# Sinkhorn-sorted attention and a max-out layer on one core: keys' block diagonal by accumulating selection matmuls, and another order of the first item's steps

## The chip, the cores and the metric

The kernel runs on one core of a Trainium2 chip. The metric is device time in microseconds (us), the median of several runs; before the change it is 168.74 us, with three runs from 168.64 to 168.83. The core has five engines that run their own instruction queues in order: TensorE (PE in the profile, with its weight loads as PEld), VectorE (DVE), ScalarE (ACT), GpSimd (POOL) and SyncE (SP). They meet through semaphores. Sixteen DMA engines move data between the chip's memory (HBM) and the on-chip memory (SBUF). Matrix products land in PSUM, which is divided here into four buffers of 128 x 1024 fp32.

## The reference

There are 4 batch items with 8 heads, 768 positions and 64 features a head. The positions are cut into 8 blocks of 96. A small matrix per head (8 x 8) is normalised by five Sinkhorn rounds, and the blocks of keys and values are mixed by it. Each block of queries then attends only to the mixed block of the same number. The result, as 3072 tokens of 512, goes through a max-out layer.

```python
P = sort_net                                   # 4 x 8 x 8 x 8
for _ in range(5):
    P = np.exp(P - max)                        # row maximum
    P = P / (P.sum(-1) + 1e-09)                # rows, then columns
    P = P / (P.sum(-2) + 1e-09)
k_sorted = einsum('bhij,bhjcd->bhicd', P, k_b) # the same for v
scores = scale * q_block @ k_sorted_block.T    # block by block
attn = softmax(scores)
x = (attn @ v_sorted_block)                    # -> 3072 x 512
out = np.maximum(x @ w1, x @ w2) @ w_out       # w1, w2: 512 x 1024
```

## The kernel before

**The max-out.** max(x w1, x w2) is written as relu(x (w1 - w2)) + x w2. So `w_difference` subtracts w2 from w1 in quarters of columns, `moe_h` makes g = relu(x (w1 - w2)) in four quarters t for each half `ch` of an item's tokens, and `out_products` adds g w_out and x (w2 w_out). The matrix w2 w_out (`wc`) is made once, by `w2_transposes` and `w_product`, during item 0.

**Sorting by matmul.** For one item the 8 x 8 matrices of 8 heads stand on a block diagonal of 64 x 64 (`bd_v` for values, `bd_k` for keys, both laid twice over 128 partitions). `sort_k` multiplies 16 columns c of keys at a time (three calls per item, 32 matmuls each), `sort_v` 16 features at a time (four calls for item 0, 16 matmuls each). Each call fills one PSUM buffer, which one copy of 1024 elements a partition evacuates, on ScalarE (L108) or VectorE (L110).

**The block diagonal.** After the last Sinkhorn round `p_bf` holds P for all 32 heads, one head a partition. `block_diagonals` spreads an item's rows to 128 partitions by one matmul with a selection of ones (`sel_k`, `sel_v`; L317), multiplies by a mask that keeps the wanted j (`maskJ`, into pm, L325), sums over j (pt, L332), and multiplies by a mask that keeps the head (`maskM`, into bd, L335). For item 0 keys and values go through these steps together. VectorE makes the selections, by copies of parts of the identity matrix.

**Per item**: `q_transposes` (two calls, 24 matmuls each), `scores` for 8 units u (8 matmuls, then an exp on ScalarE, L506), `values` for 8 units (8 matmuls, then a reciprocal and a multiply on VectorE into x, L536 and L542), four `x_transposes` (for item 0 on TensorE with an evacuation, later by DMA), eight `moe_h`, six output tiles. Units 0 to 3 belong to the first half of tokens and 4 to 7 to the second; a transpose of x takes two units.

**What sets the order.** All is in program order (a manual schedule). For item 0 the order up to `moe_h(0, 0, 1)` is written out by hand from `SC, VA, TR = att(0)` on. The rest of item 0, and the attention of the next item, run in a loop of units: each unit is one `moe_h`, `w_product` or half an output tile, and a table of tails (`first_tail` and so on) says which steps follow which unit. Where a step names no engine for its evacuation, `pick` gives it to ScalarE or VectorE by two running sums of cost. PSUM buffers are handed out in turn from the pool of four: a step waits until the buffer's last user has been read. `keep_streaming` puts matmuls of zeros ahead of a step to keep TensorE's clock up.

**Loads.** All loads of inputs but P go through GpSimd's queue, in program order: v, k and q of item 0, the weights in column pieces, then item 1's k and q, v of items 1 and 2, and so on. There are eight semaphores for them, used in turn, so the ninth load is issued when the first has landed. GpSimd also makes the identity matrix and the first two `w_difference` pieces (L205), which stand in its queue after the weight loads; the last two are VectorE's. `turn_v` puts V into the layout for sorting, on ScalarE (L222) or VectorE (L227).

Of the kernel before, what the change touches and what calls it, by code (L numbers as in the profile page):

```python
# [16 lines left out]
def kernel(  # L17
# [16 lines left out]
    nc = tc.nc  # L34
# [31 lines left out]
    def ps_f32(name):  # L66
        return psum.tile([128, 1024], FP32, tag="ps", name=name)
# [125 lines left out]
    make_identity(nc, ident)  # L193
    load_k(0)
    load_q(0, True)
    for t in range(2):
        load_w_columns(w2_sb, moe_w2, t, t + 1)
        load_w_columns(w1_sb, moe_w1, t, t + 1)
# [68 lines left out]
    def masks(part):  # L267

        if part == 0:
            nc.vector.tensor_tensor(  # L270
                out=id64, in0=ident[:, 0:64], in1=ident[:, 64:128], op=ALU.add
            )
            nc.vector.reduce_sum(
                out=maskJ[:, 0], in_=id64.rearrange("p (m j) -> p j m", j=NB), axis=AX.X
            )
            nc.vector.reduce_sum(
                out=maskM[:, 0], in_=id64.rearrange("p (m j) -> p m j", j=NB), axis=AX.X
            )
            return
        keys = id64.rearrange("p (a j ch) -> p a j ch", j=NB, ch=2)  # L280
        nc.vector.reduce_sum(
            out=maskJ[:, 1], in_=keys.transpose([0, 2, 1, 3]), axis=AX.XY
        )
        for ch in range(2):
            nc.vector.reduce_sum(
                out=maskM[:, 1, ch * 4 : ch * 4 + 4], in_=keys[:, :, :, ch], axis=AX.X
            )

    sel_v, sel_k = {}, {}

    def selections(b):
        heads = {0: (0, 1), 2: (2, 1), 3: (3, 3)}.get(b)
        if heads:
            sel_v[b] = const.tile([G, 2, 8, NB], BF16, tag=f"sel_v{b}", name="sel_v")
            for half, item in enumerate(heads):
                nc.vector.tensor_copy(
                    out=sel_v[b][:, half],
                    in_=ident[0:G, item * 8 : item * 8 + 8].to_broadcast([G, 8, NB]),
                )
        sel_k[b] = const.tile([G, 8, 16], BF16, tag=f"sel_k{b}", name="sel_k")  # L300
        nc.vector.tensor_copy(
            out=sel_k[b], in_=ident[0:G, b * 8 : b * 8 + 8].to_broadcast([G, 8, 16])
        )

    bd_v, bd_k = {}, {}

    def block_diagonals(kinds, m0=0):

        pe = ps_f32("pe")
        n = len(kinds)  # L310
        for c, (m, b) in enumerate(kinds):
            sel = (
                sel_k[b].rearrange("g h w -> g (h w)")
                if m
                else sel_v[b].rearrange("g two h j -> g (two h j)")
            )
            nc.tensor.matmul(  # L317
                pe[:, c * 64 : c * 64 + 64],
                sel,
                p_bf.rearrange("p i j -> p (i j)"),  # L320
                start=True,
                stop=True,
            )
        pm = const.tile([128, n, NB, NB], FP32, tag=f"pm{n}", name="pm")
        nc.vector.tensor_tensor(  # L325
            out=pm,
            in0=pe[:, 0 : n * 64].rearrange("p (m i j) -> p m i j", i=NB, j=NB),
            in1=maskJ[:, m0 : m0 + n].to_broadcast([128, n, NB, NB]).transpose([0, 1, 3, 2]),
            op=ALU.mult,
        )  # L330
        pt = const.tile([128, n, NB], FP32, tag=f"pt{n}", name="pt")
        nc.vector.reduce_sum(out=pt, in_=pm, axis=AX.X)  # L332
        for c, (m, b) in reversed(list(enumerate(kinds))):
            bd = const.tile([128, 8, NB], BF16, tag=f"bd{m}{b}", name="bd")
            nc.vector.tensor_tensor(  # L335
                out=bd,
                in0=maskM[:, m].to_broadcast([128, 8, NB]),
                in1=pt[:, c].to_broadcast([128, NB, 8]).transpose([0, 2, 1]),
                op=ALU.mult,
            )  # L340
            if m:
                bd_k[b] = bd.rearrange("p m i -> p (m i)")
            else:
                bd_v[b] = bd.rearrange("p m i -> p (m i)")


    v_sb = big.tile([BLK, 128, D + 16], BF16, tag="v_sb", name="v_sb")
# [169 lines left out]
    def values(b, u, n=0):  # L517
        ih, hp = divmod(u, HP)
        e = e_tiles.pop((b, u))
        m0 = (b % 2) * 64  # L520
        ps = ps_f32("o_ps")
        keep_streaming(ps, n)
        for h2 in range(2):
            for ii in range(4):
                nc.tensor.matmul(  # L525
                    ps[:, h2 * 512 + ii * 65 : h2 * 512 + (ii + 1) * 65],
                    e[:, (h2 * 4 + ii) * BLK : (h2 * 4 + ii) * BLK + 128],
                    v_sb[:, m0 + (hp + 4 * h2) * 8 + ih * 4 + ii, 0:65],
                    start=True,
                    stop=True,  # L530
                )
        ov = ps[0:BLK].rearrange("p (t f) -> p t f", t=2)[:, :, 0 : 4 * 65].rearrange(
            "p t (i f) -> p t i f", f=65
        )
        rs = xpool.tile([BLK, 2, 4], FP32, tag="rs", name="rs")
        nc.vector.reciprocal(out=rs, in_=ov[:, :, :, 64])  # L536
        if hp % 2 == 0:
            x_tiles[b, ih, hp // 2] = xpool.tile(
                [BLK, 2, 4, 2, D], BF16, tag="x", name="x", bufs=4
            )  # L540
        x = x_tiles[b, ih, hp // 2][:, :, :, hp % 2, :]
        nc.vector.tensor_tensor(  # L542
            out=x,
            in0=ov[:, :, :, 0:D],
            in1=rs.to_broadcast([BLK, 2, 4, D]),
            op=ALU.mult,
        )
        load["D"] += 900
# [70 lines left out]

    def moe_h_products(b, ch, t, hps, n=0):  # L620
        if hps[0] == 0:
            h_ps[t] = ps_f32("h_ps")
            keep_streaming(h_ps[t], n)
        for m in range(2):
            fb = t * 2 + m
            for hp in hps:
                nc.tensor.matmul(  # L627
                    h_ps[t][:, m * 512 : m * 512 + TCH],
                    w1_sb[:, hp, fb * 128 : (fb + 1) * 128],
                    xT[:, b % 2, ch, hp % 2, hp // 2, :],  # L630
                    start=(hp == 0),
                    stop=(hp == 3),
                )

    def moe_h(b, ch, t, eng=None, hps=(0, 2, 1, 3), n=0):
        moe_h_products(b, ch, t, hps, n)
        ps = h_ps[t]
        g = gpool.tile([128, 2, TCH], BF16, tag="g", name="g")
        src = ps.rearrange("p (t f) -> p t f", t=2)[:, :, 0:TCH]
        if (eng or pick((200 + 2 * TCH) / 1.2, (130 + 2 * TCH) / 0.96)) == "A":  # L640
# [62 lines left out]
    keep_streaming(ps_f32("fill_ps"), 86 * 142, most=142)  # L703
    for it in range(5):
        sinkhorn(it)
        if it < 2:
            masks(it)
        if it == 2:
            selections(0)
            turn_v(first, "A", 0, 18)  # L710
        if it == 3:
            turn_v(first, "A", 18, 36)
    turn_v(first, "A", 36, 56)
    turn_v(first, "A", 56, 80)
    block_diagonals([(0, 0), (1, 0)])
    turn_v(first, "D", 80, 96)

    SC, VA, TR = att(0)
    sort_k(0, 0, 1024, "A")
    sort_k(0, 1, 0, "D")  # L720
    sort_k(0, 2, 0, "A")
    sort_v(0, 0, 0, "D")
    sort_v(0, 1, 0, "A")
    q_transposes(0, 0, "D")
    sort_v(0, 2, 0, "A")
    sort_v(0, 3, 0, "D")
    SC[0]()
    SC[4]()
    q_transposes(0, 1, "D")
    SC[1]()  # L730
    VA[0]()
    SC[2]()
    values(0, 1, 512)
    SC[3]()
    values(0, 2, 512)
    x_transposes(0, 0, "A")
    VA[3]()
    VA[4]()
    SC[5]()
    moe_h_products(0, 0, 0, (0, 2), 512)  # L740
    x_transposes(0, 1, "A")
    SC[6]()
    VA[5]()
    moe_h(0, 0, 0, "A", (1, 3))
    SC[7]()
    VA[6]()
    moe_h(0, 0, 1, "A")
    x_transposes(0, 2, "A")
    w_difference(2)
    VA[7]()  # L750
    w2T_ready = w2_transposes(0, "D")
    w_difference(3)
    w2T_ready()
    for b in range(1, B):
        selections(b)
    for c, n, m in [(2, 2, 0), (4, 3, 1)]:
        nc.vector.tensor_copy(
            out=maskJ[:, c : c + n],
            in_=maskJ[:, m].to_broadcast([128, NB, n]).transpose([0, 2, 1]),
        )  # L760

    def turn(rows, c0):
        turn_v(rows, "D", c0, c0 + 24)
        load["D"] += 850

    load_q(1)
    for piece in range(2):
        for b in (1, 2):
            load_v(b, which=piece)
    load_k(2)  # L770

    def sorts_and_scores(b):
        SC, VA, TR = att(b)
# [4 lines left out]
    TQ = [lambda half=half: q_transposes(1, half) for half in range(2)]  # L778
    TURN = [lambda c=c: turn(both, c) for c in (0, 24, 48, 72)]
    first_tail = {  # L780
        2: [lambda: x_transposes(0, 3)],
        3: [lambda: w2_transposes(1, "A")(), lambda: load_q(2)],
        5: [lambda: block_diagonals([(0, 2), (0, 3), (1, 1), (1, 2), (1, 3)], 2)],
        7: KS,
        9: [TQ[0], TURN[0]],
        10: [SC[0], TQ[1], TURN[1]],
# [50 lines left out]
    }  # L837
    tails = [first_tail, second_tail, third_tail, {}]
    for b in range(B):
        units = [lambda t=t: moe_h(b, 0, t, None if b else "A") for t in range(4)]  # L840
        if b == 0:
            units[0] = lambda: None
            units[1] = lambda: None
        units += [lambda t=t: moe_h(b, 1, t) for t in range(4)]
        cost = [13] * 8
        if b == 0:
            units += [lambda dmt=dmt: w_product(dmt) for dmt in range(4)]
            cost += [17] * 4
# [45 lines left out]
```

## Time and profile before

Time 168.74 us; the profiled run's span is 166.8 us at a granted TensorE clock of 1.0. Busy time by stretch, from the trace:

| stretch, us | PE | DVE | ACT | POOL | what runs |
|---|---|---|---|---|---|
| 2 to 12 | 9.25 | 7.82 | 5.62 | 8.09 | Sinkhorn, zero matmuls, turning V, issuing loads |
| 12 to 20 | 7.04 | 6.80 | 6.63 | 4.03 | sorts and query transposes of item 0 |
| 20 to 25 | 4.38 | 4.01 | 3.24 | 4.50 | scores and values of item 0 |
| 25 to 30 | 4.74 | 3.18 | 4.38 | 2.95 | the same, with the first h products |
| 30 to 40 | 10.00 | 6.36 | 5.62 | 2.66 | h products of item 0 |
| 0 to 167 | 157.6 | 79.2 | 83.1 | 29.5 | all |

The columns give the microseconds in which an engine had an instruction running. Matmuls are pipelined and the records of their ends are modelled, so a full PE column says that TensorE had work at every moment, not that it ran at its peak. A chain of work, followed back from the last instruction, gives TensorE 82% of the span, VectorE 8%, ScalarE 3% and "issue" (an engine that waited for nothing the profile shows) 3%.

### The profile page before, as it was taken

The numbers are of one execution on the slowest core, as the hardware profiler recorded it, in microseconds if no ns is written. First come the engines' busy times: TensorE is split into PE (matmuls) and PEld (weight loads), VectorE is DVE, ScalarE is ACT, GpSimd is POOL, SyncE is SP. The second block draws the span as 40 slices with busy tenths as digits, with TensorE's granted clock in tenths as the row PEclk, the third lists the DMA queues.
The fourth block names the chain that finished last, engine by engine and source line by source line (L and its number), as shares of the span: only waits on it lengthen the run. The fifth ranks groups of instructions, "written<-read, shape, count | busy, mean of one in ns | idle before, by whom it ended". The sixth has DMA issues, their size and how long they took to land.

```text
span 166.8 us, 4537 instructions
## 1 busy us (share of the span) xinstructions
PE 157.6 (94%) x1993; PEld 95.7 (57%) x2011; DVE 79.2 (47%) x182; ACT 83.1 (50%) x101; POOL 29.5 (18%) x46
## 2 busy tenths in 40 slices
PE   7989799999999999999999999999999999999991
PEld 7839676766545555557555554575555545654451
DVE  4978885847484784535257774070642320000011
ACT  3587868674168627045752353467447206642010
POOL 7965587230113000000004120000000000000000
PEclk9999999999999999999999999999999999999999
DMA  3999999999999984659602999998025253000342
GB/s 43 205 205 197 199 207 206 211 203 218 207 202 215 216 219 87 173 111 173 133 0 57 160 221 169 202 250 84 2 51 173 47 173 130 0 0 0 126 155 102
DMA packets 30404, 23.90 MB, mean 143 GB/s; under 512 B 16752, under 2 KB 25200, under 8 KB 30384
## 3 DMA queue, kind: packets, MB, share of 16 engines
q0 software_dynamic: 11040, 13.37, 47.4%
q1 hardware_dynamic: 19200, 10.17, 27.1%
q8 instruction: 16, 0.26, 0.6%
q10 hardware_dynamic: 144, 0.07, 0.1%
q14 instruction: 4, 0.03, 0.1%
HBM read 26.75 MB, written 6.29 MB: 198 GB/s over the span
## 4 chain that ended last, share of the span: by engine, by line
PE 82%; DVE 8%; issue 3%; ACT 3%; DMA 1%; ACTq 0%
PE out_ps L654 34%; PE h_ps L627 25%; PE wc_ps L607 4%; PE k_ps L408 4%; PE o_ps L525 4%; PE s_ps L498 3%; PE tq_ps L383 2%; DVE x L542 1%; PE v_ps L473 1%; PE tw_ps L588 1%; ACT e L506 1%; DVE v_dc L227 1%; DMA p_sb<-in_sort_net_dram 1%; PE v_ps L429 1%; ACT xT L108 1%
## 5 line engine op out<-in xcount | busy, mean ns | idle before, releaser
L654 PE MATMUL out_ps<-wo_sb,g 128*128 128x512 bf16 (+2 forms) x187 | 46.0, 370 | 1.4 <-issue 0.9
L627 PE MATMUL h_ps<-xT,w_sb 128*128 128x384 bf16 x256 | 44.4, 326 | 0.3 <-ACT xT L108 0.3
L627 PEld LDWEIGHTS <-w_sb 128*128 128x128 bf16 x256 | 24.2, 98 | 16.1 <-issue 0.4
L506 ACT ACTIVATE e<-s_ps 96x768 bf16<-96x768 f32 x32 | 24.2, 806 | 14.9 <-PE s_ps L498 14.9
L641 ACT ACTIVATE g<-h_ps 128x768 bf16<-128x768 f32 x27 | 21.9, 811 | 17.0 <-PE h_ps L627 16.9
L654 PEld LDWEIGHTS <-g 128*128 128x128 bf16 x200 | 17.1, 97 | 15.8
L654 PE MATMUL out_ps<-wc,xT 128*128 128x512 bf16 (+2 forms) x98 | 24.7, 370 | 0.1
L108 ACT COPY o<-out_ps 128x1024 f32<-128x1024 f32 x9 | 9.1, 1012 | 28.3 <-PE out_ps L654 25.7
L542 DVE TENSOR_TENSOR x<-o_ps,rs 96x512 bf16<-96x512 f32 x32 | 22.0, 687 | 1.1
L654 PEld LDWEIGHTS <-xT 128*128 128x128 bf16 x100 | 9.6, 97 | 11.2
L525 PEld LDWEIGHTS <-e 96*128 96x128 bf16 x256 | 11.5, 97 | 5.5
L536 DVE RECIPROCAL rs<-o_ps 96x8 f32<-96x8 f32 x32 | 6.4, 201 | 16.7 <-PE o_ps L525 16.7
L689 DVE COPY o<-out_ps 128x512 f32<-128x512 f32 (+1 forms) x2 | 1.3, 626 | 27.6 <-PE out_ps L654 27.6
L525 PE MATMUL o_ps<-v_sb,e 96*128 96x65 bf16 x256 | 12.7, 193 | 0.0
L110 DVE CAST v_sb<-v_ps 96x1024 bf16<-96x1024 f32 x8 | 9.7, 1217 | 4.6 <-PE v_ps L473 3.5
L643 DVE TENSOR_SCALAR g<-h_ps 128x768 bf16<-128x768 f32 x5 | 4.8, 956 | 12.1 <-PE h_ps L627 12.1
L110 DVE CAST kT<-k_ps 128x1024 bf16<-128x1024 f32 x6 | 7.2, 1221 | 6.7 <-PE k_ps L408 6.7
L108 ACT CAST v_sb<-v_ps 96x1024 bf16<-96x1024 f32 x8 | 8.0, 1008 | 3.1 <-PE v_ps L473 1.7
L498 PE MATMUL s_ps<-qT,kT 64*128 64x96 bf16 x256 | 8.7, 204 | 0.5 <-DVE qT L110 0.4
L160 POOL DMA_DIRECT2D v_raw<-in_k_dram x3 | 2.5, 822 | 37.8 <-DVE rs L536 37.6
L498 PEld LDWEIGHTS <-kT 64*128 64x128 bf16 x256 | 6.0, 94 | 5.4 <-issue 2.2
L169 POOL DMA_DIRECT2D v_raw<-in_v_dram x11 | 5.9, 539 | 12.7 <-DVE v_dc L227 7.5
(85 smaller groups left out, 144.6 us busy)
## 6 DMA issues: line engine op xcount, KB each, us to landing
out_dram<-o SPq DMA_DIRECT2D x11, 512.0 KB, 3.0
v_raw<-in_v_dram POOLq DMA_DIRECT2D x8, 384.0 KB, 13.4
k_raw<-in_k_dram POOLq DMA_DIRECT2D x9, 256.0 KB, 10.0
w_sb<-in_moe_w_dram POOLq DMA_DIRECT2D x4, 256.0 KB, 10.1
w_sb<-in_moe_w_dram POOLq DMA_DIRECT2D x2, 512.0 KB, 11.1
wo_sb<-in_moe_w_out_dram POOLq DMA_DIRECT2D x2, 512.0 KB, 14.5
v_raw<-in_v_dram POOLq DMA_DIRECT2D x3, 256.0 KB, 4.9
q_raw<-in_q_dram POOLq DMA_DIRECT2D x4, 192.0 KB, 9.2
```

Source lines behind the costliest of these rows:

```text
L108: nc.scalar.copy(out=out_ap, in_=in_ap)
L110: nc.vector.tensor_copy(out=out_ap, in_=in_ap)
L408: nc.tensor.matmul(ps[r0 : r0 + 64, m * 64 : (m + 1) * 64], kv[r0 : r0 + 64, t * 16 + m, :], bd_k[b][r0 : r0 + 64, :], start=True, stop=True,)
L498: nc.tensor.matmul(ps[:, h2 * 512 + ii * 128 : h2 * 512 + ii * 128 + BLK], kT[b][rows, (hp * 8 + i) * BLK : (hp * 8 + i) * BLK + 128], rhs ...
L506: nc.scalar.activation(out=e[:, 0 : 8 * BLK].rearrange("p (t c r) -> p t c r", t=8, r=R), in_=ps[0:BLK] .rearrange("p (t f) -> p t f", t=8 ...
L525: nc.tensor.matmul(ps[:, h2 * 512 + ii * 65 : h2 * 512 + (ii + 1) * 65], e[:, (h2 * 4 + ii) * BLK : (h2 * 4 + ii) * BLK + 128], v_sb[:, m0 ...
L536: nc.vector.reciprocal(out=rs, in_=ov[:, :, :, 64])
L542: nc.vector.tensor_tensor(out=x, in0=ov[:, :, :, 0:D], in1=rs.to_broadcast([BLK, 2, 4, D]), op=ALU.mult,)
L607: nc.tensor.matmul(ps[:, 0:512], w2T[:, fb, dmt * 128 : (dmt + 1) * 128], wo_sb[:, fb, :], start=(fb == 0), stop=(fb == NFB - 1),)
L627: nc.tensor.matmul(h_ps[t][:, m * 512 : m * 512 + TCH], w1_sb[:, hp, fb * 128 : (fb + 1) * 128], xT[:, b % 2, ch, hp % 2, hp // 2, :], sta ...
L641: nc.scalar.activation(out=g, in_=src, func=AF.Relu)
L654: nc.tensor.matmul(dst, g_tiles[b, ch, m // 2][:, m % 2, off : off + 128] if m < NFB else xT[:, b % 2, ch, hp % 2, hp // 2, off : off + 12 ...
```

## The change

**The keys' block diagonal of item 0** is made by a function of its own, `block_diagonals_first`. For keys, eight matmuls accumulate into eight columns: the j-th takes column j of P (`p_bf[:, :, j]`) and a selection `one_j` that holds ones only for partitions of block j. The sum over j is thus done in PSUM, and one multiply by `maskM` gives bd. The values keep the way over pm and pt, after the keys' multiply. `one_j` is made by GpSimd: a memset of zeros and a copy of parts of the identity.

**The selections** of the other items move from VectorE, after the first h products, to GpSimd, ahead of the weight loads. Item 0's stays on VectorE. The mask sum for values' j moves from Sinkhorn's first round to its third, and the copies of masks for later items move ahead of item 0's sorts.

**The order of item 0** is a list of steps up to the last of its eight h products. The letter at the end names the evacuating engine (A or D), F puts 512 columns of zeros ahead of the next step; k, v, tq, SC, VA, tx, tw are the sorts, query transposes, scores, values, x transposes and w2 transposes; `h01a` is the first half of the products of half 0, quarter 1 (two of four contractions), `h01bA` the second half with the evacuation. The halves of the h products are interleaved with each other and with the values. The loads for items 1 and 2 stand inside the list, 26 steps before its end, and the load of item 2's queries after it. In the unit loop the eight h units of item 0 and three of the tails fall away, and the two cost sums start from fixed values.

```diff
+    for b in range(1, B):
+        selections(b)                      # now on GpSimd
+    one_j = const.tile([G, 8 * 130], BF16, tag="one_j", name="one_j")
+    nc.gpsimd.memset(one_j, 0.0)
+    nc.gpsimd.tensor_copy(
+        out=one_j.rearrange("g (j x) -> g j x", x=130)[:, :, 0:128].rearrange(
+            "g j (h w) -> g j h w", w=16
+        )[:, :, :, 0:2],
+        in_=ident[0:G, 0:8].to_broadcast([G, 8, 2, NB]).transpose([0, 3, 1, 2]),
+    )
...
+    def block_diagonals_first():
+        pe = ps_f32("pe")
+        for j in range(NB):
+            nc.tensor.matmul(pe[:, 0:NB], one_j[:, j * 128 : (j + 1) * 128],
+                             p_bf[:, :, j], start=(j == 0), stop=(j == NB - 1))
+        nc.tensor.matmul(pe[:, 512:576], sel_v[0], p_bf, start=True, stop=True)
+        # bd_k[0] = maskM[:, 1] * pe[:, 0:NB]
+        # pm = pe[:, 512:576] * maskJ[:, 0]; pt = sum over j
+        # bd_v[0] = maskM[:, 0] * pt
...
-    block_diagonals([(0, 0), (1, 0)])
+    block_diagonals_first()
     turn_v(first, "D", 80, 96)
...
-    sort_k(0, 0, 1024, "A")
-    sort_k(0, 1, 0, "D")
-    sort_k(0, 2, 0, "A")
-    sort_v(0, 0, 0, "D")
-    ...
+    front = """
+        k0D k1A k2D v1D v2A v3A tq0D v0A tq1D SC1 SC0 F1
+        SC2 VA1 SC5 VA0 SC3 F2 VA2 SC4 F0 tx0D SC6 VA3
+        SC7 h00a VA4 tx1A tw0D h01a VA5 h01bA diff2 h00bA VA7 tx2A
+        tw1A h02a VA6 h02bA h11a diff3 tx3A h12a h03a h12bD h10a h10bA
+        pe2 h11bD h03bA h13a h13bA
+    """.split()
...
     first_tail = {
-        2: [lambda: x_transposes(0, 3)],
-        3: [lambda: w2_transposes(1, "A")(), lambda: load_q(2)],
-        5: [lambda: block_diagonals([(0, 2), (0, 3), (1, 1), (1, 2), (1, 3)], 2)],
         7: KS,
...
         if b == 0:
-            units[0] = lambda: None
-            units[1] = lambda: None
+            units, cost = [lambda: None] * 8, [0] * 8
```

## The prediction

> **What bounds the kernel now.** I read the page's slices first: they say which engine is full in which stretch.
>
> ```profile
> PE   7989799999999999999999999999999999999991
> DMA  3999999999999984659602999998025253000342
> ```
>
> A slice is 4.2 us. TensorE is full from the sixth slice on, so a change to the first item's steps can only win time that TensorE loses before that. The 16 DMA engines are full for the first 14 slices (58 us): what is loaded there lands at times that an earlier request doesn't move. Next comes the chain that ended last, in order of time (start, duration, what):
>
> ```profile
> 11.39 0.23 PE pe L317 x2
> 11.64 0.30 DVE pm L325
> 11.96 0.30 DVE pt L332
> 12.28 0.24 DVE bd L335
> 12.56 1.71 PE k_ps L408 x96
> ...
> 16.86 1.02 ACT v_sb L108
> ...
> 18.82 0.97 DVE qT L110
> 19.84 0.36 PE s_ps L498 x8
> 20.20 0.30 issue
> ...
> 22.70 0.81 ACT xT L108
> ...
> 24.95 0.81 ACT xT L108
> ...
> 30.02 1.30 PE h_ps L627 x8
> ...
> 39.41 1.64 PE k_ps L408 x96
> ```
>
> Until 30 us the chain leaves TensorE for evacuations; after it there is TensorE alone. From the keys' sort (12.56) to that of item 1 (39.41) are 26.85 us. TensorE's work in it, from rows of the same chain: sorts 1.64 + 4 x 0.52, query transposes 1.75, scores and values 16 x 0.24, x transposes 4 x 0.34, h 8 x 1.30, w2 transposes 2 x 0.89, selection 0.25, fillers 3 x 0.22: 23.7 us. So 3.1 us are idle, and no order of these steps wins more. Last, the timeline, for what the DMA holds back:
>
> ```profile
> 17.77 2.21 ACT L506 ACTIVATE e<-s_ps 96x768 bf16<-96x768 f32 x3
> ...
> 19.67 2.12 POOL L205 TENSOR_TENSOR w_sb<-w_sb 128x1024 bf16<-128x1024 bf16 x1 [1.84 <-DMA w_sb<-in_moe_w_dram]
> ...
> 48.65 1.59 DVE L227 COPY v_dc<-v_raw 128x768 uint32<-128x768 uint32 x2 [0.77 <-ACT e L506]
> ...
> 52.19 1.13 PE L473 MATMUL v_ps<-bd,v_dc 64*128 64x64 bf16 x48
> ```
>
> The first weights land at 19.7. The turn of V's second half waits at 48.65; the named exp isn't an operand of it, so I read this as its load landing. It ends at 50.24, and the sort that needs it starts at 52.19: 1.9 us of slack, the second ceiling.
>
> **What the Trainium skill says.** "SBUF — State Buffer", Who interferes with whom: a VectorE instruction with two SBUF inputs contends with a GpSimd instruction that reads SBUF, and the later one waits for the whole of the other. Before, GpSimd reads SBUF only in the differences at 19.7 and 22.3; the multiplies of x beside them take 0.69 us like all others, but have only one SBUF input, so the trace doesn't test it. "GPSIMD Engine Reference", section 3.1: about 1 cycle an element for one input, 2.6 for two, at 1.2 GHz; the two-input difference, 1024 elements in 2.12 us, agrees (2.5 cycles). "TensorE: Matmul & The Clock Gate", Back-to-back issue gap: however small, matmuls don't start closer than 25 ns; the value sorts show 33 ns (32 in 1.04 us).
>
> **The change, part by part.** *Keys' block diagonal.* Eight accumulating matmuls of 8 columns replace one of 64. At 33 ns each the group (nine with the values' one, whose end the block diagonal also waits for) ends 7 x 0.033 = 0.23 us later, so VectorE starts at 11.87, not 11.64. But what starts there is already the keys' block diagonal: pm and pt (0.32 + 0.32 between starts) aren't ahead of it. It starts 0.41 us earlier than 12.28. Bounds: 25 ns gives 0.47, the 56 ns of the w2 transposes (16 in 0.89) gives 0.25.
>
> *The price of its selection.* GpSimd makes one_j after seven selection copies, from 7.95 on, when it has issued q's loads. The trace shows no copy there; near are a memset of 128 elements (0.23) and the mask's select (0.32). I take 0.3 for the three copies of 128, 0.22 for the four of 64, 1.0 for the memset of 1040, 0.3 for one_j: 3.1 us, ready at 11.05. Ends: 2.3 and 4.1 us, ready at 10.25 or 12.05. TensorE wants it at 11.4. Meanwhile sinkhorn's multiplies (0.21 us, both inputs in SBUF) at 8.60 and 9.36 meet the copies: half a copy each, 0.2 us in all (0 to 0.6), which also pushes GpSimd. I take 0.2 for the contention and 0.1 for lateness: the start wins 0.41 - 0.3 = 0.1. Moving the mask sums costs nothing net: 0.13 less in the first iteration, which waits for VectorE (4.61 against an exp done at 4.42), about as much more in the third.
>
> *Weights requested later.* GpSimd's first weight load is issued at 11, not 8.49; the fifth still waits for q (14.48). Costed at nothing: k and q are queued ahead until 17 us, and the DMA never runs dry.
>
> *New order to the scores.* The keys' block diagonal at 12.17, then on VectorE 0.14 to the next, pm and pt at half the old size (0.24 each between starts), bd 0.14, the turn 0.54, the two maskJ copies 0.2 (moved here from 32.6, where they were free): k0 is evacuated from 13.67, k2 from 14.84 (two in 2.35) to 16.06, v1 to 17.2. The query transposes take k2's PSUM buffer: 16.1, plus 0.16 and 0.79, to 17.05; v0 to 17.57, the second half of queries to 18.4. Score 1 starts there, its exp 0.38 later (as 19.84 to 20.22): 18.78. That is 1.0 us later than the first exp before.
>
> *New order after them.* But now the eight exps stand on ScalarE with nothing between: the first x transpose's and w2's evacuations went to VectorE, the other x transposes behind the exps. At 0.74 each (three in 2.21) the last ends at 24.8, against 28.2. Scores need the buffers that exps free, so the eighth group waits for the sixth exp: 18.78 + 5 x 0.74 + 0.81 = 23.3. From there half h products (0.65 each) stand between the values, and I find every input ready when TensorE arrives: first difference at 21.8, second at 24.4 for an h at 25.7, third on VectorE at 28.7 (its load landed by 27.8) for an h at 29.3. Only the fourth x transpose waits 0.1 for ScalarE's 1.87 us evacuation of w2T. TensorE's work from the eighth scores on: 0.24 + h 8 x 1.30 + values 4 x 0.24 + x transposes 3 x 0.34 + w2 2 x 0.89 + selection 0.25 = 14.65. Item 1's keys sort starts at 23.3 + 14.65 + 0.1 = 38.1, not 39.41: 1.3 us.
>
> *Behind it.* Item 1's keys landed by 36.4 and its queries by 41.6 (needed at about 43.2), so both loads still come in time; the V sort would start at 50.9, still after 50.3. Selections for the other items leave VectorE, where nothing waited. A few evacuations change sides later (five of eight value sorts on ScalarE); buffers still come free in time. From item 1's values on the order is the same, so the 1.3 us stay: 168.74 - 1.3 = 167.4.
>
> **The rivals.** *A dear start.* GpSimd takes 4.1 us plus 0.4 of contention, one_j is ready at 12.45, the block diagonal starts near 12.9, 0.65 late. The order wins 1.2; 0.55 stays: 168.2. For it: no GpSimd copy was ever seen here and the margin is 0.35 us. Against: two bounds must meet.
> *The ceiling.* GpSimd is early and contends with nothing; the start wins 0.4, and unseen slack the rest up to V's landing: 1.9, so 166.9. For it: the earlier stages allow 3.1. Against: the exps' pace is fixed.
> *Slower.* The chain shows 0.30 us of "issue" at 20.20, after scores that waited for queries, which no operand explains. If six of the stalled groups in the new order pay it, 1.8 us go: 0.5 slower, 169.2. The first exp is late by 1 us already, and each exp waits for scores that wait for an exp. Against: it shows once in the old order, though others stalled there too.
>
> **How the numbers follow.** Forecast (167.4) 0.56, dear start 0.20, ceiling 0.12, slower 0.12. The range, 166.8 to 168.6, takes in the ceiling and the dear start, and leaves out the slower case and the worst of GpSimd's costs. Faster by over 0.2% means under 168.40: nearly all of the forecast, the ceiling, and two thirds of the dear start: 0.79. Within: 0.10. Slower: 0.11.
>
> **What would show it.** The profile after should have the keys' bd near 12.2, with one_j's copy on GpSimd done by 11.4; the first exp near 18.8 and the eighth done by 25; no TensorE idle from the eighth scores on; item 1's k_ps at 38.1; V's second turn still at 48.65. It is wrong if the nine matmuls wait for GpSimd, if sinkhorn's multiplies grow beyond 0.21 us by more than 0.3 in all, if gaps of 0.3 us stand before scores or values, or if VectorE, with two more evacuations among the x, makes an x transpose late.

## The result, and the profile after

After the change the kernel takes 167.31 us (median; 167.10 to 167.76), beside 168.69 for the kernel before: a ratio of 0.9921, with a 95% interval of 0.9899 to 0.9944. A second set of runs (r1 below) gave 166.93 (166.85 to 167.67) beside 168.71: 0.9904, 0.9889 to 0.9919. So 1.4 to 1.8 us are won. Slow executions, with a lower granted TensorE clock and a time over 1.5% above the fastest of their kernel, are left out of all medians, ranges and ratios here.

The page's slices of the profiled execution (167.39 us, span 165.6):

```profile
PE   7999899999999999999999999999999999999992
DMA  3999999999999996698403999997025283000333
```

The third slice of TensorE shows a 9 where it was 8 and the fifth an 8 where it was 7; from the sixth on it was full already. The DMA engines are full for 14 slices as before. The chain that ended last, in order of time (start, duration, what):

```profile
9.56 2.54 PE fill_ps L82 x11
12.10 0.30 PE pe L367 x8
...
12.98 1.64 PE k_ps L469 x96
...
18.77 0.97 DVE qT L110
19.78 0.35 PE s_ps L559 x8
...
20.49 0.27 issue
20.76 0.34 PE s_ps L559 x8
...
27.30 1.30 PE h_ps L688 x8
...
38.82 1.64 PE k_ps L469 x96
...
75.43 1.64 PE k_ps L469 x96
...
108.85 1.64 PE k_ps L469 x96
...
162.60 0.27 ACT o L748
```

Two things are new. From 20.76 to item 1's keys sort (38.82, before 39.41) the chain is TensorE alone; before, it left TensorE between 21 and 26 for VectorE's x and for two evacuations. And at its head stands, ahead of the selection matmuls (pe), TensorE's own queue of zeros.

The kernel before has these two sorts and its last copy at:

```profile
76.12 1.64 PE k_ps L408 x96
...
109.67 1.64 PE k_ps L408 x96
...
163.41 0.27 ACT o L687
```

So item 1's keys sort starts 0.59 us earlier, and that is not half of the 1.23 us between the two profiled executions (168.62 and 167.39). From there to item 2's keys sort (76.12; 75.43) and on to item 3's (109.67; 108.85) another 0.10 and 0.13 are won. From item 3's sort to ScalarE's last copy both take 53.7 us. The other 0.42 comes behind the last copy: before, the span goes on for 3.43 us, after for 3.01. GpSimd's four semaphore instructions at the program's end, before and after, show where:

```profile
L889 POOLq EVENT_SEMAPHORE  x4: 17/17/17, 165.7 to 166.7; - x4
```

```profile
L958 POOLq EVENT_SEMAPHORE  x4: 17/17/17, 164.9 to 165.5; - x4
```

From the first to the last of them are 1.05 us before and 0.63 after. All work of the kernel is over by then.

The timelines of ScalarE, VectorE and TensorE:

```profile
19.05 6.00 ACT L567 ACTIVATE e<-s_ps 96x768 bf16<-96x768 f32 x8
...
48.62 2.30 DVE L257 COPY v_dc<-v_raw 128x768 uint32<-128x768 uint32 x3
...
51.60 1.13 PE L534 MATMUL v_ps<-bd,v_dc 64*128 64x64 bf16 x48
```

All eight exps run without a gap and end at 25.05 (before 28.16). VectorE's last turns of V begin at 48.62 where they began at 48.65, but for another reason: three of them now follow directly behind another copy, where before the last two had waited 0.77 us.

The start, on GpSimd and VectorE:

```profile
9.34 0.95 POOL L218 MEMSET one_j<- 32x1040 bf16 x1
10.36 0.29 POOL L219 COPY one_j<-ident 32x128 bf16<-32x128 bf16 x1
```

```profile
8.34 0.31 DVE L280 TENSOR_TENSOR p_sb<-p_sb,rowsum 32x64 f32<-32x64 f32 x1
...
9.20 0.27 DVE L285 TENSOR_TENSOR p_sb<-p_sb,colsum 32x64 f32<-32x64 f32 x1
...
11.02 0.21 DVE L285 TENSOR_TENSOR p_bf<-p_sb,colsum 32x64 bf16<-32x64 f32 x1
12.48 0.22 DVE L382 TENSOR_TENSOR bd<-maskM,pe 128x64 bf16<-128x64 f32 x1 [1.26 <-PE pe L374]
```

one_j is there at 10.65 and P at 11.23. Neither is what the matmuls of 12.10 wait for: VectorE is idle for 1.26 us because TensorE is still at its zeros. The first lines of TensorE's timeline say why, in before, in this execution, and in the second run of the changed kernel:

```profile
1.19 6.78 PE L82 MATMUL fill_ps<-fill 128*128 128x142 bf16 x86 [1.19 <-DVE fill L73]
```

```profile
1.20 8.31 PE L82 MATMUL fill_ps<-fill 128*128 128x142 bf16 x86 [1.20 <-DVE fill L73]
```

```profile
1.20 7.38 PE L82 MATMUL fill_ps<-fill 128*128 128x142 bf16 x86 [1.20 <-DVE fill L73]
...
11.32 0.36 PE L367 MATMUL pe<-p_bf,one_j 32*128 32x8 bf16 x8 [0.15 <-DVE p_bf L285]
```

The same 86 matmuls take 6.8 to 8.3 us from one execution to the next. By the starts of the single matmuls, TensorE begins one every 0.119 us at first and one every 0.062 us later. The change comes at 4.0 us in before and at 7.2 in this execution. With 8.31 us the zeros of the last two Sinkhorn rounds (6 matmuls each) push the selection back; with 7.38 it waits for p_bf alone.

### The profile page after: what moved, and what is told of

It reads as the page before. It is cut to its first block, busy times and chain, and to the rows that moved or that the text cites. A ratio compares the mean times of both kernels' runs of the same rounds, so it can differ in the third digit from the quotient of the medians.

```text
span 165.6 us, 4544 instructions
## 1 busy us (share of the span) xinstructions
PE 158.8 (96%) x2000; PEld 97.2 (59%) x2018; DVE 76.6 (46%) x173; ACT 83.1 (50%) x102; POOL 32.2 (19%) x55
## 4 chain that ended last, share of the span: by engine, by line
PE 85%; DVE 7%; issue 3%; ACT 2%; DMA 1%; ACTq 0%
PE out_ps L715 33%; PE h_ps L688 26%; PE o_ps L586 4%; PE wc_ps L668 4%; PE k_ps L469 4%; PE s_ps L559 4%; PE tq_ps L444 2%; PE fill_ps L82 2%; ACT e L567 1%; PE v_ps L490 1%; PE v_ps L534 1%; PE tw_ps L649 1%; DVE v_dc L257 1%; DMA p_sb<-in_sort_net_dram 1%; PE tx_ps L624 1%
## 5 line engine op out<-in xcount | busy, mean ns | idle before, releaser
L108 ACT COPY o<-out_ps 128x1024 f32<-128x1024 f32 x10 | 10.1, 1012 | 28.3 <-PE out_ps L715 25.6
L110 DVE CAST kT<-k_ps 128x1024 bf16<-128x1024 f32 x7 | 8.3, 1217 | 6.3 <-PE k_ps L469 6.3
L108 ACT CAST v_sb<-v_ps 96x1024 bf16<-96x1024 f32 x10 | 9.8, 1015 | 2.5 <-PE v_ps L490 0.9
L82 PE MATMUL fill_ps<-fill 128*128 128x142 bf16 x86 | 8.3, 283 | 1.2 <-DVE fill L73 1.2
L110 DVE CAST v_sb<-v_ps 96x1024 bf16<-96x1024 f32 x6 | 7.3, 1217 | 4.5 <-PE v_ps L534 2.2
L82 PEld LDWEIGHTS <-fill 128*128 128x128 bf16 x91 | 8.5, 127 | 1.4 <-DVE fill L73 1.2
```

The lines of the kernel that those rows point to most:

```text
L82: nc.tensor.matmul(ps[:, 0:w], w0, fill[:, 0:w], start=True, stop=True)
L108: nc.scalar.copy(out=out_ap, in_=in_ap)
L110: nc.vector.tensor_copy(out=out_ap, in_=in_ap)
```

## The experiments

For each kernel one profiled execution (its time in the third column) and the median of several. Start times in us: item 0's keys sort; TensorE going on after a stop near 20 us (below); the eighth score group; item 1's keys sort, by the timeline (the chain shows it 0.07 later).

| kernel | median | profiled | keys 0 | after the stop | scores 8 | keys 1 |
|---|---|---|---|---|---|---|
| before | 168.69 | 168.62 | 12.56 | 20.50 | 26.55 | 39.34 |
| after | 167.31 | 167.39 | 12.91 | 20.76 | 23.79 | 38.75 |
| e1_old_diagonal | 167.56 | 167.27 | 12.70 | 20.77 | 23.68 | 38.63 |
| e2_old_order | 169.04 | 169.10 | 12.77 | 20.50 | 26.83 | 39.62 |
| e3_fewer_zeros | 167.15 | 166.55 | 12.14 | 19.98 | 22.97 | 37.93 |
| e4_no_F | 167.34 | 167.19 | 12.59 | 20.51 | 23.48 | 38.44 |
| r1_changed_again | 166.93 | 166.93 | 12.19 | 20.24 | 23.27 | 38.23 |
| s1_scalar_evacuations | 167.51 | 167.48 | 12.24 | 20.51 | 23.54 | 38.84 |
| s2_halves_together | 168.65 | 168.47 | 12.57 | 20.25 | 23.37 | 39.84 |
| e5_before_fewer_zeros | 168.40 | 168.39 | 12.58 | 20.50 | 26.25 | 39.04 |
| s3_spread_exponentials | 168.73 | 168.84 | 12.21 | 20.51 | 26.65 | 40.03 |
| c2_old_diagonal_fewer_zeros | 167.75 | 167.78 | 12.51 | 20.79 | 23.45 | 38.42 |
| c3_fewer_zeros_again | 167.06 | 167.06 | 12.14 | 20.52 | 23.46 | 38.42 |
| c1_late_selections | 167.44 | 167.18 | 12.07 | 20.47 | 23.41 | 38.38 |

The profiled time less the last column is 128.62 to 128.81 us in ten of the twelve kernels that have the new steps; e2 (129.48) and c2 (129.36) are told of under c2. So what is won by item 1's keys sort is kept to the end. Before and e5 have 129.3, so about 0.65 us of every gain in the table come from behind that sort. Of it the first 0.10, up to item 2's keys sort, goes with the order: before, e2 and e5 take 36.71 us there, all others 36.61. The 0.42 at the end doesn't: it is there in all twelve, in e2 with the old order, in e1 and c2 without one_j. Only before and e5 lack it, and they alone have neither the moved selections nor the moved mask sums. Why the end gets shorter by them is open.

### The two halves of the change

**e1_old_diagonal**: the new order with the old way to both block diagonals (no one_j; item 0's key selection on VectorE).

```diff
-    block_diagonals_first()
+    block_diagonals([(0, 0), (1, 0)])
```

> The changed kernel, but item 0's keys' block diagonal made the old way (one selection matmul each for keys and values, then pm, pt and bd for both); one_j is left out, the new order stays. If the accumulating matmuls shorten the path to the first sort, as the prediction has it, the keys' bd starts 0.4 to 0.5 us later after the selection matmuls' start than in the changed kernel, and the time is 167.3 + 0.4 = 167.7. Rival, that the start isn't on the path because the exps or VectorE's evacuations set the pace: no difference, 167.3. Rival, that GpSimd's one_j and its contention eat the gain: 167.1 to 167.3.

Measured 167.56, ratio 0.9931 (0.991 to 0.9951). Without the new diagonal nearly all of the gain stays, and the interval overlaps that of the whole change. This isn't the order alone: the moved selections and mask sums are still in it, and with them the 0.42 us at the end.

**e2_old_order**: the kernel before with the new start alone (one_j, selections on GpSimd, the moved mask sums, `block_diagonals_first`).

```diff
+    for b in range(1, B):
+        selections(b)                  # on GpSimd, and one_j
...
-    block_diagonals([(0, 0), (1, 0)])
+    block_diagonals_first()
```

> The kernel before, with the new start alone (accumulating matmuls, one_j and selections on GpSimd, masks moved), and item 0's old order. If the order carries most of the gain (about 1.0 of 1.4 us): 168.2 to 168.4. Rival, that the start carries it: 167.3 to 167.6. Rival, that the start costs more than it gives on its own: 168.7 to 168.9.

Measured 169.04 (168.05 to 170.06), ratio 1.0012 (0.9986 to 1.0038). The start alone wins nothing that can be measured. In the profiled execution the zeros ended late (8.18 us for the first 86), keys' sort began 0.2 later than in the kernel before, and item 1's keys sort 0.28 later; the 0.42 at the end is won here too, and lost again on the way.

### What of the order wins

**s1_scalar_evacuations**: in the new order, the first x tile and the first w2T tile are evacuated by ScalarE.

```diff
-        SC2 VA1 SC5 VA0 SC3 F2 VA2 SC4 F0 tx0D SC6 VA3
-        SC7 h00a VA4 tx1A tw0D h01a VA5 h01bA diff2 h00bA VA7 tx2A
+        SC2 VA1 SC5 VA0 SC3 F2 VA2 SC4 F0 tx0A SC6 VA3
+        SC7 h00a VA4 tx1A tw0A h01a VA5 h01bA diff2 h00bA VA7 tx2A
```

> The changed kernel with the copies of the first x tile and of the first w2T tile on ScalarE (0.80 and 1.86 us there) in place of VectorE (0.55 and 1.22). Theory (the order gains because the eight exponentials have ScalarE to themselves): the copy of the first x tile stands ahead of the last two exponentials, which end 0.8 later, the PSUM buffers that they release too, and the copy of w2T stands ahead of two relus: keys' sort of item 1 0.4 to 0.9 later, 167.7 to 168.2. Rival (TensorE has other work ready in any case, so who evacuates doesn't matter): 167.2 to 167.5.

Measured 167.51, ratio 0.9933 (0.9916 to 0.9949), beside 166.93 (0.9904) for the changed kernel: 0.6 us slower by the medians, though the intervals touch. ScalarE's timeline shows what was expected:

```profile
23.07 0.79 ACT L108 COPY xT<-tx_ps 128x768 bf16<-128x768 bf16 x1
23.75 1.52 ACT L567 ACTIVATE e<-s_ps 96x768 bf16<-96x768 f32 x2
...
26.41 1.87 ACT L108 COPY w2T<-tw_ps 128x2048 bf16<-128x2048 bf16 x1 [0.21 <-PE tw_ps L649]
```

The copy stands ahead of the last two exps, but only 0.34 us of it reach item 1's keys sort (18.33 us from the stop's end to it, 17.99 in r1); the other 0.27 of the profiled difference was the stop's. So ScalarE's freedom matters, and in this one execution it is the smaller part.

**s2_halves_together**: each first half of an h product directly ahead of its second half, all else the same.

```diff
-        SC7 h00a VA4 tx1A tw0D h01a VA5 h01bA diff2 h00bA VA7 tx2A
-        tw1A h02a VA6 h02bA h11a diff3 tx3A h12a h03a h12bD h10a h10bA
-        pe2 h11bD h03bA h13a h13bA
+        SC7 VA4 tx1A tw0D VA5 h01a h01bA diff2 h00a h00bA VA7 tx2A
+        tw1A VA6 h02a h02bA diff3 tx3A h12a h12bD h10a h10bA
+        pe2 h11a h11bD h03a h03bA h13a h13bA
```

> The changed kernel with each h product's first half moved down to directly ahead of its second half, all else in the same order. If the interleaving of the halves fills waits of its own for the x tiles (0.2 to 0.4 us of them at the second and third x tile): 167.5 to 167.8. If the gain is from the exponentials alone and the interleaving only keeps TensorE occupied where other work would do: 167.2 to 167.4.

Measured 168.65, ratio 1.0008 (0.9994 to 1.0023): all of the gain is gone, far outside both expectations. At item 1's keys sort (39.84) it is even 0.5 us behind the kernel before; the 0.65 behind that sort hides this. Its chain:

```profile
23.71 0.70 DVE x L603
...
24.46 0.51 PE tx_ps L624 x8
...
29.56 0.69 ACT xT L108
30.25 1.85 ACT w2T L108
32.09 0.71 ACT g L702
32.81 0.70 ACT xT L108
...
33.55 2.11 PE h_ps L688 x12
...
39.91 1.64 PE k_ps L469 x96
```

The eight exps still run without a gap and end at 24.63, and the eighth scores start at 23.37, earlier than in the profiled execution of the changed kernel. But with no half products between, TensorE stands at the second x transpose for VectorE's multiply, and then ScalarE's row of copies and relus (28.7 to 33.5) sets the pace up to the fourth x tile. In 24 to 39 us TensorE is busy 13.79 of 15 us, against 15.00 in the changed kernel. From the eighth scores to item 1's keys sort it takes 16.47 us instead of 14.96. This is one list with the halves together; whether another choice of evacuating engines would make it faster isn't shown.

**s3_spread_exponentials**: the other way round: scores and evacuations in the order of before, the halves interleaved where their inputs allow. The new list (the old one is cut here):

```diff
+        k0D k1A k2D v1D v2A v3A tq0D v0A SC0 SC4 tq1D SC1 F1
+        VA0 SC2 VA1 SC3 F2 VA2 tx0A VA3 VA4 SC5 h00a tx1A
+        h01a SC6 VA5 h00bA SC7 VA6 h01bA diff2 tx2A VA7 h02a tw0D
+        h02bA tw1A h11a diff3 tx3A h12a h03a h12bD h10a h10bA
+        pe2 h11bD h03bA h13a h13bA
```

> The changed kernel with the order of the kernel before up to the eighth score group (score groups 0, 4, 1, 2, 3, 5, 6, 7; copies of the first two x tiles and a relu between the exponentials on ScalarE), and the h halves still interleaved wherever their x tiles allow. Theory (both are needed: with the halves together the early exponentials were worth nothing, and with late exponentials the last x tiles come too late for the halves to fill the waits): the eight exponentials end at 27 to 28, keys' sort of item 1 starts at 39.0 to 39.6, 168.0 to 168.6. Rival (the interleaving alone is enough, since it gives TensorE something to do in every wait): keys' sort at 38.0 to 38.6 and 166.8 to 167.4.

Measured 168.73, ratio 0.9999 (0.998 to 1.0019); the exps end at 28.26 and item 1's keys sort starts at 40.03. Interleaving alone wins nothing either: by item 1's keys sort it is 0.7 us behind the kernel before. From its chain:

```profile
27.82 0.57 issue
28.39 0.69 DVE w_sb L235
...
29.12 0.82 PE h_ps L688 x4
...
32.42 1.87 ACT w2T L108
...
34.34 2.81 PE h_ps L688 x16
```

The last values and x tiles come late, so their copies and the weights' difference meet on the evacuating engines when TensorE has run out of half products. This list is one of many with late exps, and its place for `diff2` costs a part of it; that another with late exps would be as slow isn't shown.

### The start, and a stop near 20 us

**e3_fewer_zeros** and, run a second time, **c3_fewer_zeros_again**: 2048 columns of zeros in place of 3072 in each of the last two Sinkhorn rounds.

```diff
-            keep_streaming(ps_f32("fill_ps"), 3072, it)
+            keep_streaming(ps_f32("fill_ps"), 2048, it)
```

> The changed kernel with 2048 instead of 3072 columns of zeros in each of the last two Sinkhorn rounds. In the changed kernel's trace TensorE ran zeros until 12.10 us although P was ready at 11.23, because its clock rose 3 us later than in the trace of the kernel before. If that queue of zeros sets the start, the selection matmuls come at 11.3 whenever the clock rises, and the time falls by up to 0.8 us in executions that warm late and by nothing in those that warm early: 166.6 to 167.1, with less spread. Rival, that the zeros end in time in most executions: 167.3. Rival, that fewer zeros let the clock fall: 168 or more.

> The changed kernel with 2048 columns of zeros again, as the measure for the two kernels beside it: 166.5 to 167.2. If the zeros were what made one execution of the changed kernel differ from the next, its times lie closer together than 166.8 to 167.8.

Measured 167.15 (0.9891, 0.9857 to 0.9926) and 167.06 (0.9878, 0.985 to 0.9907). The zeros no longer stand in the way: in c3 the first 86 took 7.78 us, and still the selection begins with P and bd at 11.71. But that isn't kept whole. TensorE's timeline in c3:

```profile
19.67 0.26 PE L559 MATMUL s_ps<-qT,kT 64*128 64x96 bf16 x4
20.52 0.26 PE L559 MATMUL s_ps<-qT,kT 64*128 64x96 bf16 x4 [0.59 <-issue]
```

In the middle of a score group, with all operands there, TensorE stands for 0.59 us. This is the "issue" gap that the prediction saw at 20.20 and built its slower rival on. Its place in the old start with the old order (before), and in the new start with the old order (e2):

```profile
20.50 0.39 PE L82 MATMUL o_ps<-fill 128*128 128x512 bf16 x1 [0.32 <-PE s_ps L498]
```

```profile
20.05 0.21 PE L558 MATMUL s_ps<-qT,kT 64*128 64x96 bf16 x1 [0.43 <-DVE qT L110]
20.50 0.34 PE L558 MATMUL s_ps<-qT,kT 64*128 64x96 bf16 x7 [0.24 <-issue]
```

Counted in program order, it always stands behind TensorE's 351st matmul: before, behind the eighth of score group 2 (86 + 12 zeros, 2 selections, 2 zeros, 96, 64 + 25 + 24 for v and q, 32 of scores, 8 of values). (Of the 12 zeros the trace of before holds 11; a few records are missing.) Seven more selection matmuls (e2) move it seven matmuls up the list, into that group behind its first; in the new order four fewer zeros (c3) move it four further down. Each trace shows it once, whoever waited there. And it ends at 19.98, 20.24 to 20.25, 20.47 to 20.52 or 20.76 to 20.79, while TensorE starts its 351st matmul between 19.6 and 20.4. So it costs little where TensorE comes late or the end comes early (0.05 us in e5 and 0.2 in e3, by the starts of the matmuls around it), 0.27 of idle time in the profiled execution of the changed kernel, and 0.45 to 0.7 where TensorE was early (e1, r1, s1, s3, c1, c2, c3). In the kernels with after's steps (after, e1, e3, e4, r1, c1 to c3), item 1's keys sort follows its end at 17.6 to 18.0 us.

The traces point at a cause. The page lists a DMA queue of the kind "instruction":

```profile
q8 instruction: 16, 0.26, 0.6%
```

In each of the fourteen profiles one of its packets of 16 KB starts between 17.52 and 18.39 us and takes 0.89 to 0.97, and the stop ends 2.28 to 2.53 us after that start: 17.52 and 19.98 in e3, 17.81 and 20.24 in r1, 18.08 and 20.50 in before, 18.35 and 20.76 in after. The stop's end moves with the packet, so TensorE most likely waits for instructions. This is argued from times that go together: no run moves the packet, and why no like stop follows the packet before it or the one after isn't shown.

**r1_changed_again**: the changed kernel, unaltered.

> The changed kernel again, unaltered, beside the others. If TensorE's stream of zeros sets the start (theory), the time should lie between 166.6 and 167.8 and follow from one execution to the next the moment at which TensorE's rate rises: with the initial zeros over by about 7 us the selection matmuls stand near 11.3, with 8.3 us near 12.1, and keys' sort of item 1 follows 0.6 to 0.8 later in the second kind. Rival (the start doesn't vary, the spread is the end's): keys' sort of item 1 at 38.8 whatever the zeros took.

Measured 166.93; four of its five times lie at 166.85 to 166.97, one at 167.67. With 7.38 us for the first zeros, the selection at 11.32 and keys' sort at 12.19, 0.72 earlier than in the first profile; of it 0.52 reach item 1's keys sort, which is exactly by how much the stop ended sooner (20.24 for 20.76).

**c2_old_diagonal_fewer_zeros**: e1 with 2048 columns, so that the two diagonals are compared with no zeros in the way.

```diff
-            keep_streaming(ps_f32("fill_ps"), 3072, it)
+            keep_streaming(ps_f32("fill_ps"), 2048, it)
...
-    block_diagonals_first()
+    block_diagonals([(0, 0), (1, 0)])
```

> The changed kernel with the old way to both block diagonals and 2048 columns of zeros in place of 3072, so that neither kernel's start waits for zeros. Against the changed kernel with 2048 columns in the same call. Theory (the new diagonal saves its two VectorE steps wherever zeros don't hide it): 0.3 to 0.5 slower than that kernel, 166.9 to 167.4. Rival (the start's saving is lost before keys' sort of item 1): within 0.1 of it.

Measured 167.75 (0.9921, 0.9891 to 0.995) beside c3's 167.06: 0.7 by the medians, with overlapping intervals. In the profiled executions keys' sort starts 0.37 later than in c3, as expected: 0.06 because P comes later, 0.31 behind the first selection matmul. But c3 loses it at the stop, and at item 1's keys sort both stand at 38.42. Most of the 0.7 us between those two executions has another source, in c2's chain:

```profile
96.25 12.30 DMA v_raw<-in_q_dram
...
108.57 1.03 DVE q_pair L408 x2
...
109.62 4.96 DMA qT<-q_pair
...
114.72 0.52 PE s_ps L549 x16
```

The last item's queries landed 1.1 us later than in c3 (108.57 for 107.45), and its scores waited 0.42 for their transposes; from item 3's keys sort to the last copy it takes 0.5 us longer than c3. In e2's profiled execution these scores waited too, for 0.22. So the start's worth in the whole time stays uncertain: 0.4 at the first sort, between nothing and 0.5 at item 1's keys sort.

**e4_no_F**: the changed kernel without the three F fillers.

```diff
-        k0D k1A k2D v1D v2A v3A tq0D v0A tq1D SC1 SC0 F1
-        SC2 VA1 SC5 VA0 SC3 F2 VA2 SC4 F0 tx0D SC6 VA3
+        k0D k1A k2D v1D v2A v3A tq0D v0A tq1D SC1 SC0
+        SC2 VA1 SC5 VA0 SC3 VA2 SC4 tx0D SC6 VA3
```

> The changed kernel without the three fillers of 512 columns of zeros among the scores and values. Each holds TensorE for 0.2 to 0.3 us. If the eight exps set the pace there, they stand in waits and little is won, 0 to 0.3 us: 167.0 to 167.3. Rival, that TensorE sets the pace: 0.65 us faster, 166.7. Rival, that the clock falls without them: slower than 168, with a lower rate of the matmuls after 19 us.

Measured 167.34, ratio 0.9925 (0.9906 to 0.9945): no gain to be seen. From the stop's end to item 1's keys sort are 17.93 us, with two fillers and one score matmul less to do, where the changed kernel has 17.99: the fillers lie in waits.

**e5_before_fewer_zeros**: the kernel before with 2048 columns.

> The kernel before with 2048 columns of zeros in place of 3072 in each of the last two Sinkhorn rounds. If the zeros hold up the old start as well whenever the clock rises late (theory): 168.3 to 168.6, 0.1 to 0.4 below the kernel before. Rival (they stand in waits there, and only the earlier end of the new diagonal meets them): within 0.1 of it.

Measured 168.40, ratio 0.9991 (0.9978 to 1.0004): not told apart from no change. In its profile the start is that of before (12.58), but four matmuls fewer put the stop, by the count, into a values group three matmuls further on. It still ends at 20.50, but TensorE has done a filler and three values matmuls more by then, so that only 0.05 us are lost in place of 0.32, and item 1's keys sort comes 0.30 earlier. So the gain, if there is one, isn't from the zeros' time, as the theory had it, but from where their number puts the stop.

**c1_late_selections**: 2048 columns, and GpSimd's copies for items 1 to 3 behind its weight differences.

```diff
-    for b in range(1, B):
-        selections(b)
     one_j = const.tile([G, 8 * 130], BF16, tag="one_j", name="one_j")
...
     w_difference(1, nc.gpsimd)
+    for b in range(1, B):
+        selections(b)
```

> The changed kernel with 2048 columns of zeros, and GpSimd's selection copies for items 1 to 3 behind its two weight differences, so that only the memset and the copy of one_j stand ahead of the weight requests and beside the Sinkhorn rounds. Theory (contention with GpSimd's small copies lengthens the Sinkhorn multiplies by 0.16): the start 0.1 to 0.2 earlier, 166.4 to 167.0. Rival (the copies cost nothing there, and now lie beside other VectorE work): within 0.1 of the kernel without the move, or slower.

Measured 167.44 (166.72 to 168.19), 0.9904 (0.9867 to 0.994): no faster. The profile shows the contention gone (both multiplies 0.21 us) and bd at 11.64 instead of 11.71, so 0.07 us, of which 0.04 is left at item 1's keys sort, less than what the stop's end differs by (20.47 and 20.52). No version here beats the changed kernel by more than the intervals.

## Why the prediction came out right

The time was right, and in part by luck. The prediction put all of its 1.3 us ahead of item 1's keys sort and nothing behind it. By the chain that sort starts 0.59 us earlier in the first profiled execution and 1.11 in r1. Behind it 0.64 and 0.58 are won, 0.42 to 0.44 of them at the program's end, which the prediction didn't look at. What fell short in front and what came unforeseen behind nearly made up for each other.

- **The order (1.3 us forecast).** Right in kind and too large in size: item 1's keys sort at 38.82 (after) and 38.30 (r1) by the chain, forecast 38.1; no idle TensorE from the eighth scores on (15.00 of 15 us); eight exps in 6.00 us. The stretch behind the eighth scores took 14.96 us by the timeline, forecast 14.75; the rest of what is missing in the first execution is the late start. The prediction named the exps' freedom on ScalarE as the cause and treated the half h products as what merely stands between. In the two lists that undo one of them (s2, s3) the other alone is worth nothing: early exps make the x tiles early, and the halves give TensorE work until their copies are through.
- **Nothing behind it (0 forecast).** "From item 1's values on the order is the same" holds, but two stretches got shorter all the same: 0.10 and 0.13 up to item 3's keys sort, and 0.42 behind the last copy. The first 0.10 goes with the order, perhaps with the evacuations that changed sides; this isn't shown. The last goes with the moved selections and mask sums (e2 has it, before and e5 don't), and its cause is open.
- **The ceiling of 3.1 us idle.** It fell by about half, by the busy time between the two keys sorts: 26.85 - 25.43 = 1.4 us idle before, 25.84 - 25.20 = 0.6 after. These windows count fillers and the records' overlap as busy, so they are smaller than the 3.1 from work alone; the order can't win much more.
- **The block diagonal (0.41 earlier, 0.25 to 0.47).** Right in size: from the first selection matmul to bd are 0.43 us in c3 (11.28 to 11.71), against 0.89 in before (11.39 to 12.28), so 0.46. The eight matmuls stand 26 ns apart (11.28 to 11.49), not 33; the Trainium skill's "TensorE: Matmul & The Clock Gate", Back-to-back issue gap, gives 25. What the forecast left out: the keys' sort keeps only 0.31 of it, as its own two matmuls of zeros end at 12.15, behind bd.
- **GpSimd (3.1 us, one_j at 11.05).** The size was off, on the safe side: 2.77 us from 7.88 to 10.65. So no lateness, and the dear start is refuted. A gain was left out: the copy of item 0's key selection on VectorE (0.17 us between starts, at 7.94 before) went away as well.
- **Contention (0.2).** The two multiplies took 0.31 and 0.27 instead of 0.21: 0.16. The Trainium skill's "SBUF — State Buffer", Who interferes with whom, is borne out in that only these two, beside GpSimd's copies, are longer, and both are 0.21 again in c1, where the copies are elsewhere. By how much goes with when a multiply starts among the copies: the first takes 0.30 to 0.31 where it starts at 8.34 to 8.36 (after, e3, s2) and 0.21 to 0.24 where it starts at 8.41 to 8.73 (the other eight kernels with copies there). A wait for the whole of another instruction (0.3) isn't seen.
- **bd at 12.17.** Failed twice over. Without zeros in the way it comes at 11.64 to 11.76; in the first profile at 12.48, since the prediction held zeros to be free filler, when they are a queue ahead of the selection and their end moves with TensorE's early rate.
- **Scores at 18.4, first exp at 18.78.** 18.3 for the exp in early executions (c3, e3, r1), 19.05 in the first. What an early one wins, up to 0.5 us, it loses at the stop near 20 us, which the prediction read as a price of stalled groups. It isn't: the gap comes once, at a fixed count of matmuls. That refutes the slower rival (no six gaps) and also the ceiling rival's early start, which can't be carried past it.
- **V's landing as second ceiling.** Not met, but near: its sort starts at 51.60, and at 50.77 in e3, the fastest execution, where the last turn of V had waited for its load and ended at 50.40. That the turns in after begin near the forecast 48.65 is chance. The ceiling that did show was another, the last item's queries (c2, e2).
- **Weights later, mask moves.** As forecast: the first difference runs at 19.56 and none of the h products waits for one.

## What to carry to other kernels

An earlier input to a chain of stages and more work for the engine that waits in it can each be worth nothing and together be worth the gain, as here in the lists tried; when a reordering does both, undo each by itself before naming the cause. A total that comes out as forecast can be two misses: compare forecast and trace stretch by stretch, to the program's last instruction. Zeros that keep TensorE busy are a queue like any other: ask when it ends in several executions, not only in the one profiled. And a gap that no operand explains should be located by instruction count in two kernels that differ in it, before a cost is laid on it.

## What the hardware showed unexpectedly

- The moment at which TensorE's rate rises varies: the same 86 matmuls of zeros took 6.78, 6.86, 6.87, 6.89, 7.38, 7.38, 7.53, 7.61, 7.66, 7.78, 7.98, 7.99, 8.18 and 8.31 us in the fourteen profiles. The Trainium skill's "TensorE: Matmul & The Clock Gate", Part 1, has TensorE at half its rate for about 3.4 us of work. Half the rate agrees (0.119 and 0.062 us a matmul), the time doesn't always: work begins at 1.2 us here, and the rate rose at 4.0 us in before and at 7.2 in after, behind 2.8 and 6.0 us of work.
- The stop ahead of the 352nd matmul, 0.05 to 0.7 us, whose end follows a 16 KB packet of an instruction queue at 2.28 to 2.53 us in all fourteen profiles. That the packet is its cause is argued, not shown.
- The program's end behind the last copy took 3.42 to 3.43 us in before and e5 and 2.99 to 3.01 in the twelve others; why is open.
- On 32 partitions GpSimd took 0.28 to 0.37 us for a copy of 128 bf16 elements, 0.40 to 0.47 for two of 64, and 0.95 to 1.04 for a memset of 1040.
- A load of 768 KB (the last item's queries) took 12.3 us from issue in one execution (c2) and 11.3 in another (c3), and behind it c2 fell back by about 0.5 us.
